# TensorE in written order through three of five MoE groups, local attention heads in joint stretches at fixed steps

## The chip, the cores and the metric

The kernel runs on one core of one Trainium2 chip. The metric is the device time of one execution in microseconds, as the median of several executions. The core's engines are TensorE (PE in the profile, with PEld for its weight loads), VectorE (DVE), ScalarE (ACT), GpSimd (POOL), and SyncE (SP), which issues the DMAs.

## The reference

Sparse attention over 4 batches, 8 heads, 576 positions and head size 64 is followed by two MoE-like blocks without routing. Four heads are local (a position sees the 32 up to itself), four are strided (it sees the earlier positions with the same residue modulo 32).

```python
mask_local = (rel >= 0) & (rel < stride)
mask_strided = (rel >= 0) & (pos[None, :] % stride == pos[:, None] % stride)
scores = np.where(masks[None, :, :, :], scores, -1000000000.0)
scores = scores - np.max(scores, axis=-1, keepdims=True)
attn = np.exp(scores)
attn = attn / (np.sum(attn, axis=-1, keepdims=True) + 1e-09)
out = np.matmul(attn, v)                                   # B, H, S, D

x = out.transpose(0, 2, 1, 3).reshape(B * S, H * D)        # 2304 x 512
h = x @ w_in                                               # first MoE block, d_ff 2048
x = (h - np.tanh(h)) @ w_out

rms = np.sqrt(np.mean(x * x, axis=-1, keepdims=True) + 1e-06)
xn = x / rms * rms_g                                       # second MoE block, d_ff 1536
g = xn @ w_gate
y = (g / (1.0 + np.exp(-g)) * (xn @ w_val)) @ w_out        # 2304 x 512
```

## The kernel before, in words

The 2304 tokens are cut into nine blocks of 256, numbered 0 to 8, and the blocks into five groups: (0, 1), (2, 3), (4), (5, 6), (7, 8). A group is 512 tokens wide, the middle one 256. While one group goes through the first MoE block, the attention of the next group's blocks is computed beside it; the last group has none beside it and prepares the second MoE block.

**The MoE step.** Group g takes 16 steps f (`unit`, L839). TensorE computes 12 matmuls into ps_h (`pe_h`, L643), ScalarE the tanh into tg, VectorE h minus tanh (tg, L659), ScalarE the high part of g (L665), VectorE its low part (g, L670), and TensorE 12 matmuls into ps_x (`pe_x`, L672) two steps later. ps_h has two buffers: the matmuls of step f + 2 wait for tg of step f. At the end of a group ps_x is evacuated (xe, L689 on VectorE, L691 on ScalarE).

**The local heads.** Each block has two units (`Local`, L218) and each unit three stages on TensorE. Stage s makes the scores (ps_s); VectorE then masks them and takes the maximum (L299, four times), ScalarE takes the exponential (L307), and VectorE normalises (ss, L311 and L312, and sm, L314). Stage p transposes the result (ps_p, L328), and ScalarE copies it out (L331). Stage v multiplies by the values (ps_v), and the result goes to the group's input xs, high part on ScalarE (L355), low part on VectorE (L356).

**The strided heads** of blocks 4 to 8 need no TensorE (`Strided`, L452). In a qk stretch GpSimd multiplies queries with keys into pr (L486) and VectorE sums each product into sc (L491). A softmax follows (smx, se, L501 to L509, with ScalarE's exponential at L505). In a pv stretch GpSimd multiplies with the values (L519), VectorE sums into so (L526), transposes (L534) and writes the low part into xs (L545) after ScalarE's high part (L544). pr has two buffers, so GpSimd is at most two products ahead of VectorE. Keys, queries and values have one buffer each. Block 4 has four short qk and pv stretches, one for each batch; blocks 5 and 6 have their qk in one long run, and then their pv; block 7 has one of each, and block 8.

**What sets the order.** The program is written step by step. In `unit`, `pe_work` stands between tanh and tg and takes stages from the list of the next group's local heads (`Work.run_pe`, L629), and `work` takes strided items (`Work.run`, L618). In the three middle groups `run_pe` is called with the number of steps that remain:

```python
def run_pe(self, k):
    n = -(-len(self.pe) // k) if k > 0 else len(self.pe)
    for _ in range(min(n, len(self.pe))):
        self.pe.pop(0)()
```

So one stage of one unit is written per step from step 0 on, in the order s, p, v of unit 0, then of unit 1. A scheduler then puts the instructions of every engine into an order of its own, from a simulated timeline. On the chip each engine takes its instructions in that order and waits at each for what it needs.

Of the kernel before, what the change touches and what calls it, by code (L numbers as in the profile page):

```python
# [25 lines left out]
def attn_moe_moe_kernel(  # L26
# [37 lines left out]
    NG = len(groups)  # L64
# [3 lines left out]
    def runs(s):  # L68

        r = []  # L70
        for i, (b, t) in enumerate(subs[s]):
            if r and r[-1][0] == b and r[-1][1] + r[-1][2] == t:
                r[-1][2] += 64
            else:
                r.append([b, t, 64, 64 * i])
        return r

    LB = 2
    EA = 2
    GC = 2  # L80
    PR = 6 * 64
    LANES = (5, 6, 7, 8)
# [22 lines left out]
    for s in range(len(subs)):  # L105
        if len(runs(s)) > 1 or s in LANES:
            _, t0, n, _ = runs(s)[0]
# [9 lines left out]
    class Weight:  # L117
        def __init__(self, kind, f):
            self.kind, self.f = kind, f
# [86 lines left out]
    def room(j, pool, name, words=512, **kw):  # L206

        if j < EA:
            return wts.tile([128, 1024], F32, tag="w", name=name)
        return pool.tile([128, words], F32, name=name, **kw)  # L210

    def copy(j, i):
        if j < EA and "aavaaaaa"[4 * j + i] == "v":
            return nc.vector.tensor_copy
        return nc.scalar.copy


    class Local:  # L218
# [9 lines left out]
        def load_qk(self):  # L228
            if self.j < EA:
                self.kT = wts.tile([128, 1024], F32, tag="w", name="kT")[:, :2 * self.kw]  # L230
                self.kT = self.kT.rearrange("r (p t) -> r p t", p=2)
                self.qz = wts.tile([128, 1024], F32, tag="w", name="qz").rearrange("r (u p t) -> r u p t", p=2, t=128)
                (nc.vector if self.j == 0 else nc.gpsimd).memset(self.qz[0:64, :, :, 64:128], 0.0)
                nc.gpsimd.memset(self.qz[64:128, :, :, 0:64], 0.0)
            else:
                self.kT = one.tile([128, 2, 4 * (W + 64)], F32, tag="kT", name="kT")[:, :, :self.kw]
                self.qz = qz
                if self.j == EA:
                    nc.gpsimd.memset(qz, 0.0)
            for b, t0, n, x0 in self.runs:  # L240
                for hh in range(2):
                    r = slice(64 * hh, 64 * hh + 64)
                    nc.sync.dma_start(
                        out=self.qz[r, x0 // 64:(x0 + n) // 64, :, r].rearrange("r u p t -> r (u p) t"),
                        in_=q_loc[b, r, t0 // 32:(t0 + n) // 32, :],
                    )
                o = self.at[x0 // 64]
                d = W if t0 == 0 else 0
                nc.sync.dma_start(out=self.kT[:, :, o + d:o + W + n], in_=k_loc[b, :, :, t0 - W + d:t0 + n])
# [112 lines left out]
    class Dense:  # L362
# [6 lines left out]
        def buf(self, tag, name, words):  # L369
            if self.j < EA:  # L370
                return wts.tile([128, 1024], F32, tag="w", name=name)
            return one.tile([128, words], F32, tag=tag, name=name)
# [79 lines left out]
    class Strided:  # L452
# [16 lines left out]
        def items(self):  # L469
# [5 lines left out]
            def flush():  # L475
                while pend:
                    pend.pop(0)()

            def prod(n, d):
                pr = att.tile([128, PR], F32, tag="pr", name="pr", bufs=2)  # L480
                return pr[:, :n * d].rearrange("l (c d) -> l c d", d=d)
# [31 lines left out]
            def pv_item(c, a, e, g0, gn):  # L513
                def go():
                    if c == g0 and a == 0:
                        flush()
                        self.o = one.tile([128, GC, D], F32, tag="so", name="so")
                    pr = prod(c + 1, e - a)
# [40 lines left out]
            qks.append((4, soft))  # L559
            for g0 in range(c0, c1, GC):  # L560
                gn = min(GC, c1 - g0)
                for c in range(g0, g0 + gn):
# [6 lines left out]
    loc = [Local(j) for j in range(len(subs))]  # L569
# [8 lines left out]
    class Work:  # L578


        def __init__(self, js):
            self.pe, self.st = [], []
            for j in js:
                pools = [(ps_m, "m"), (ps_h, "h")] if j < 1 else [(ps_m, "m")]
                kinds = [loc[j]]
                if isinstance(strd[j][0], Dense):
                    kinds += strd[j]
                else:
                    for o in strd[j]:
                        self.st += o.pvs if j in EARLY else o.items().qks + o.pvs  # L590
                    if j + 1 == EARLY[0]:
                        for o in (strd[i][0] for i in EARLY):
                            self.st += o.items().qks
                for nms in ("s,p,v" if j < EA else "spv").split(","):
                    for i in range(2):
                        for nm in nms:
                            for o in kinds:
                                self.pe.append(self.stage(o, i, nm, pools[len(self.pe) % len(pools)]))
# [28 lines left out]
                fn()  # L627

        def run_pe(self, k):  # L629
            n = -(-len(self.pe) // k) if k > 0 else len(self.pe)  # L630
            for _ in range(min(n, len(self.pe))):
                self.pe.pop(0)()


    def new_x(g):
        if g < NG:
            xs[g] = mid.tile([128, 2, 4, 512], F32R, tag="xs", name="xs")
            for k, j in enumerate(groups[g]):
                xh[j] = xs[g][:, :, :, SUB * k:SUB * k + SUB]
# [236 lines left out]
    for g, f, a, e in units:  # L876
        if g == 0:
            st1.to(2 * (f + 4))
        elif f == 0:
            new_x(g + 1)  # L880
            if g + 1 < NG:
                wks.append(Work(groups[g + 1]))
        if g == NG - 1 and f == 0:
            poolT.close()
            pbx = ctx.enter_context(tc.tile_pool(name="pbx", bufs=1, side="right", reuse_waits="tile"))
            gcol = pbx.tile([128, 4], F32, name="gcol")
            nc.sync.dma_start(out=gcol, in_=rms_g.rearrange("(c p) -> p c", p=128))
            ones = pbx.tile([128, 128], F32R, name="ones")
            nc.vector.memset(ones.bitcast(F32), 1.0)
        rem = FA - 1 - f  # L890
        wk = wks[-1]

        def pe_work():
            if f >= 2 or 0 < g < NG - 1:
                wk.run_pe(max(rem, 1))

        def work():
            if f >= 6 or 0 < g < NG - 1:
                wk.run(wk.st, max(rem, 1))

        unit(g, f, a, e, pe_work, work)
        if g == NG - 1:
            if f == 4:
                pg = prep(0, pbx)
            if pg is not None:
                next(pg, None)
# [109 lines left out]
```

## Time and profile before

| | us |
|---|---|
| median of 3 runs | 943.58 (943.53 to 944.5) |
| the profiled execution, its own time | 945.95 |
| its span in the profile | 943.1 |
| busy in the span: PE | 914.2 (97%) |
| DVE | 596.8 (63%) |
| ACT | 338.4 (36%) |
| POOL | 188.6 (20%) |

The span runs from the first to the last recorded instruction; the profiled execution took 2.85 us more than its span, and 2.37 us more than the median. Busy time is a sum over the whole span. POOL works only in its first half, and DVE is busier there than its share of the whole says; so the views by stretch of time are read beside the totals.

### The profile page before, as it was taken

To read this page: it belongs to the slowest core of one execution; us is meant where nothing else is said; L and a number is where in the kernel's file an instruction comes from. 1 tells how busy PE (TensorE), PEld (TensorE's weight loads), DVE (VectorE), ACT (ScalarE), POOL (GpSimd) and SP (SyncE) were. 2 spreads that over 40 slices of the span, in tenths; PEclk is the share of its full clock that TensorE was granted. 3 is DMA by queue.
4 is the path that set the end of the run, shared out by engine and by line. 5 is a ranking of instruction groups with operands and counts; after the bars stand their busy time and mean duration, and the time that the engine had idled before them with its cause. 6 is when DMAs were issued, how large, how long until landed. Compare 5 with 4: busy or idle time off the path is not lost.

```text
span 943.1 us, 13108 instructions
## 1 busy us (share of the span) xinstructions
PE 914.2 (97%) x4922; PEld 767.5 (81%) x4922; DVE 596.8 (63%) x1315; ACT 338.4 (36%) x778; POOL 188.6 (20%) x230
## 2 busy tenths in 40 slices
PE   6799999999889999999999999999999999999998
PEld 6688887888888877788888888888888888888897
DVE  4799997887899997959999782262125312421212
ACT  4776753322333432256656332222111211111211
POOL 2000024668856757500000000000000000000000
PEclk9799999999999999999999999999999999999999
DMA  9926424421312400065535201101010001000100
GB/s 216 339 112 214 122 73 132 123 80 35 107 36 63 89 27 5 1 223 179 174 107 188 90 23 45 44 4 42 1 45 0 23 1 45 1 0 1 46 1 22
DMA packets 47839, 72.62 MB, mean 77 GB/s; under 512 B 20768, under 2 KB 31392, under 8 KB 47776
## 3 DMA queue, kind: packets, MB, share of 16 engines
q1 hardware_dynamic: 47776, 71.80, 24.8%
q8 instruction: 38, 0.62, 0.3%
q14 instruction: 25, 0.20, 0.1%
HBM read 62.34 MB, written 9.44 MB: 76 GB/s over the span
## 4 chain that ended last, share of the span: by engine, by line
PE 57%; DVE 5%; POOL 2%; issue 1%; ACT 0%; POOLq 0%; DVEq 0%
PE ps_x L113 21%; PE ps_h L113 20%; PE ps_m L113 16%; DVE so L526 2%; POOL pr L486 1%; POOL pr L519 1%; DVE tg L659 1%; DVE g L670 1%; DVE sc L491 0%; DVE xs L545 0%; DVE sm L299 0%; DVE pr L534 0%; DVE sm L314 0%; DVE os L796 0%; ACT g L665 0%
## 5 line engine op out<-in xcount | busy, mean ns | idle before, releaser
L113 PE MATMUL ps_h<-xs,w 128*128 128x512 f32 (+1 forms) x984 | 222.1, 370 | 3.3 <-DVE tg L659 2.0
L113 PE MATMUL ps_x<-g,w 128*128 128x512 f32 (+1 forms) x984 | 218.1, 367 | 1.7 <-DVE xe L689 1.5
L113 PEld LDWEIGHTS ps_h<-xs,w 128*128 128x128 f32 x984 | 170.6, 191 | 33.6 <-DVE tg L659 3.1
L113 PEld LDWEIGHTS ps_x<-g,w 128*128 128x128 f32 x984 | 169.5, 189 | 32.2 <-issue 1.4
L771 DVE SCALAR_TENSOR_TENSOR s<-ps_m,s 128x512 f32<-128x512 f32 (+1 forms) x60 | 38.2, 637 | 219.8 <-PE ps_m L113 218.5
L113 PE MATMUL ps_h<-xn,w 128*128 128x512 f32 (+1 forms) x720 | 159.0, 369 | 0.0
L113 PE MATMUL ps_m<-xn,w 128*128 128x512 f32 (+1 forms) x720 | 158.6, 368 | 0.0
L113 PE MATMUL ps_x<-w,p 128*128 128x512 f32 x648 | 157.9, 391 | 0.0
L113 PEld LDWEIGHTS ps_h<-xn,w 128*128 128x128 f32 x720 | 126.8, 188 | 24.4
L113 PEld LDWEIGHTS ps_m<-xn,w 128*128 128x128 f32 x720 | 125.9, 188 | 23.1
L113 PEld LDWEIGHTS ps_x<-w,p 128*128 128x128 f32 x648 | 120.7, 188 | 25.6
L486 POOL TENSOR_TENSOR pr<-sk,sq 128x320 f32<-128x320 f32 (+2 forms) x104 | 98.5, 980 | 73.2 <-DMA sq<-in_q_str_dram 60.6
L519 POOL TENSOR_TENSOR pr<-sv,se 128x288 f32<-128x288 f32 (+11 forms) x108 | 83.1, 780 | 65.8 <-DVE so L526 31.3
L770 ACT ACTIVATE s<-ps_h 128x512 f32<-128x512 f32 (+1 forms) x60 | 33.3, 555 | 160.7 <-PE ps_h L113 160.7
L526 DVE TENSOR_REDUCE so<-pr 128x16 f32<-128x288 f32 (+12 forms) x108 | 81.5, 771 | 11.1 <-POOL pr L519 9.9
L665 ACT CAST g<-tg 128x512 fp32r<-128x512 f32 (+1 forms) x82 | 46.6, 568 | 116.2 <-DVE tg L659 116.0
L773 ACT CAST p<-s 128x512 fp32r<-128x512 f32 (+1 forms) x60 | 34.7, 578 | 120.7 <-DVE s L771 120.7
L491 DVE TENSOR_REDUCE sc<-pr 128x5 f32<-128x320 f32 (+2 forms) x104 | 50.9, 494 | 17.9 <-POOL pr L486 17.4
L670 DVE TENSOR_TENSOR g<-tg,g 128x512 fp32r<-128x512 f32 (+1 forms) x82 | 58.1, 708 | 5.3 <-ACT g L665 4.7
L133 ACT ACTIVATE ca<-raw 128x512 f32<-128x512 f32 x68 | 45.7, 674 | 39.5 <-DVE ct L141 14.5
L774 DVE TENSOR_TENSOR p<-s,p 128x512 fp32r<-128x512 f32 (+1 forms) x60 | 38.2, 637 | 25.1 <-ACT p L773 24.9
L659 DVE SCALAR_TENSOR_TENSOR tg<-ps_h,tg 128x512 f32<-128x512 f32 (+1 forms) x82 | 50.3, 614 | 5.1 <-ACT tg L654 5.0
(87 smaller groups left out, 703.0 us busy)
## 6 DMA issues: line engine op xcount, KB each, us to landing
raw<-in_w_out_dram SPq DMA_DIRECT2D x28, 512.0 KB, 5.6
raw<-in_w_in_dram SPq DMA_DIRECT2D x16, 512.0 KB, 7.8
raw<-in_w_gate_dram SPq DMA_DIRECT2D x12, 512.0 KB, 3.5
raw<-in_w_val_dram SPq DMA_DIRECT2D x12, 512.0 KB, 4.1
x2d<-xe SPq DMA_DIRECT2D x36, 128.0 KB, 2.4
x<-x2d SPq DMA_DIRECT2D x16, 256.0 KB, 4.1
out_dram<-o SPq DMA_DIRECT2D x16, 256.0 KB, 2.0
v<-in_v_loc_dram SPq DMA_DIRECT2D x14, 192.0 KB, 2.7
```

The source lines that it names most:

```text
L113: nc.tensor.matmul(out_, lhsT, rhs, start=start, stop=stop, skip_group_check=True)
L133: nc.scalar.mul(out=a, in_=hi.bitcast(F32), mul=2.0 ** -111)
L486: nc.gpsimd.tensor_tensor(out=pr, in0=self.k[:, a:e, :], in1=self.q[:, c - c0:c - c0 + 1, :].to_broadcast([128, e - a, D]), op=ALU.mult,)
L491: pend.append(lambda: nc.vector.tensor_reduce(out=s[:, c - c0, a:e], in_=pr, axis=AX.X, op=ALU.add))
L519: nc.gpsimd.tensor_tensor(out=pr, in0=self.v[:, 0:c + 1, a:e], in1=self.e[:, c - c0, 0:c + 1].unsqueeze(2).to_broadcast([128, c + 1, e - a ...
L526: pend.append(lambda: nc.vector.tensor_reduce(out=o[:, c - g0, a:e], in_=pr.rearrange("l c d -> l d c"), axis=AX.X, op=ALU.add))
L659: nc.vector.scalar_tensor_tensor(out=t, in0=h_of.pop((g, f, a)), scalar=WS, in1=t, op0=ALU.mult, op1=ALU.subtract)
L665: nc.scalar.copy(out=t[:, 0], in_=t_of[g, f, a])
L670: nc.vector.tensor_tensor(out=t[:, 1], in0=t_of.pop((g, f, a)), in1=t[:, 0].bitcast(F32), op=ALU.subtract)
L771: nc.vector.scalar_tensor_tensor(out=s, in0=r[1], scalar=WS, in1=s, op0=ALU.mult, op1=ALU.mult)
L773: nc.scalar.copy(out=t[:, 0], in_=s)
L774: nc.vector.tensor_tensor(out=t[:, 1], in0=s, in1=t[:, 0].bitcast(F32), op=ALU.subtract)
```

## The change

From the first step of the second group to the first step of the fifth, TensorE's instructions keep the order in which they are written; the other engines are ordered by the scheduler as before. For blocks 4 to 8 (`NEAR = 4`) a block's local heads are three entries in the list, each with both units: s of both, p of both, v of both. They are written at the steps that `STINT` names, and at no other: in the second group (block 4) steps 5, 8 and 11, in the third (blocks 5 and 6) steps 1, 4, 6 and 8, 11, 13, in the fourth (blocks 7 and 8) steps 1, 3, 5 and 8, 10, 12. No instruction of any engine is added or taken away.

```diff
+    NEAR = 4
+
+    STINT = {1: (5, 8, 11), 2: (1, 4, 6, 8, 11, 13), 3: (1, 3, 5, 8, 10, 12)}
...
+                if j >= NEAR:
+                    for nm in "spv":
+                        self.pe.append(lambda o=loc[j], nm=nm: [self.stage(o, i, nm, pools[0])() for i in range(2)])
+                    continue
                 for nms in ("s,p,v" if j < EA else "spv").split(","):
...
         def run_pe(self, k):
-            n = -(-len(self.pe) // k) if k > 0 else len(self.pe)
+            n = -(-len(self.pe) // k) if k > 0 else 0
...
         elif f == 0:
+            if g == 1:
+                order = ctx.enter_context(ExitStack())
+                order.enter_context(tc.manual_schedule(engines={mybir.EngineType.PE}))
+            if g == NG - 1:
+                order.close()
             new_x(g + 1)
...
         def pe_work():
-            if f >= 2 or 0 < g < NG - 1:
+            if g in STINT:
+                wk.run_pe(len(wk.pe) if f in STINT[g] else 0)
+            elif f >= 2:
                 wk.run_pe(max(rem, 1))
```

Three places of the engines' orders follow. First TensorE at the start of the second group, before (ps_h and ps_x are the MoE step, ps_s, ps_p and ps_v the stages of a local unit; one entry may stand for two records of the trace):

```order
L113 MATMUL ps_h<-xs,w 128x512 x12
L113 MATMUL ps_s<-kT,qz 128x96 x4
L113 MATMUL ps_h<-xs,w 128x512 x12
L113 MATMUL ps_x<-g,w 128x512 x12
L113 MATMUL ps_h<-xs,w 128x512 x12
L113 MATMUL ps_x<-g,w 128x512 x6
L113 MATMUL ps_h<-xs,w 128x512 x2
L328 MATMUL ps_p<-tab,sm 96x128 x4
L113 MATMUL ps_h<-xs,w 128x512 x4
L113 MATMUL ps_x<-g,w 128x512 x6
L113 MATMUL ps_h<-xs,w 128x512 x6
L113 MATMUL ps_x<-g,w 128x512 x6
```

And with the change, from step 4 of the group on:

```order
L116 MATMUL ps_h<-xs,w 128x512 x12
L116 MATMUL ps_x<-g,w 128x512 x12
L116 MATMUL ps_h<-xs,w 128x512 x12
L116 MATMUL ps_s<-kT,qz 128x96 x8
L116 MATMUL ps_x<-g,w 128x512 x12
L116 MATMUL ps_h<-xs,w 128x512 x12
L116 MATMUL ps_x<-g,w 128x512 x12
```

The stages no longer stand inside or between pieces of a block of 12; the scores of both units stand together behind the ps_h matmuls of step 5. With the change, every block of 12 in the three groups is whole.

Second, VectorE early in the third group, where the qk of block 6 ends and the pv of block 5 begins, before:

```order
L659 SCALAR_TENSOR_TENSOR tg<-ps_h,tg 128x256
L689 TENSOR_SCALAR xe<-ps_x 128x512
L491 TENSOR_REDUCE sc_96<-pr 128x5
L670 TENSOR_TENSOR g<-tg,g 128x256
L491 TENSOR_REDUCE sc_96<-pr 128x5
L689 TENSOR_SCALAR xe<-ps_x 128x512
L491 TENSOR_REDUCE sc_96<-pr 128x5
L491 TENSOR_REDUCE sc_96<-pr 128x6
L526 TENSOR_REDUCE so<-pr 128x32
L501 TENSOR_REDUCE smx<-sc_96 128x8
```

And with the change (the score operations of the two units, eight pairs, end with the first two rows; line numbers after the change are 3 to 12 higher):

```order
L302 ISA sm,nm<-ps_s,tab 128x96
L302 ISA nm 128x1
L494 TENSOR_REDUCE sc_96<-pr 128x5
L696 TENSOR_SCALAR xe<-ps_x 128x512
L314 TENSOR_SCALAR ss<-ss 128x4
L696 TENSOR_SCALAR xe<-ps_x 128x512
L494 TENSOR_REDUCE sc_96<-pr 128x6
L315 RECIPROCAL ss<-ss 128x4
L529 TENSOR_REDUCE so<-pr 128x32
L314 TENSOR_SCALAR ss<-ss 128x4
L504 TENSOR_REDUCE smx<-sc_96 128x8
L317 TENSOR_TENSOR sm<-sm,ss 128x384
```

Before, one unit's score operations stood some rows earlier and the other's came in the pv stretch; now both units of block 5 stand between the last sums of the qk stretch, and their normalisation among the first so. All the way back to the tg of that step there are four sc in both orders.

Third, VectorE where the strided work of block 8 ends, before, from the tg of step 14 of the fourth group on:

```order
L659 SCALAR_TENSOR_TENSOR tg<-ps_h,tg 128x512
L526 TENSOR_REDUCE so<-pr 128x21
L526 TENSOR_REDUCE so<-pr 128x22
L670 TENSOR_TENSOR g<-tg,g 128x512
L534 STREAM_TRANSPOSE pr<-so 128x128
L545 TENSOR_TENSOR xs<-pr,xs 128x2x64
L889 MEMSET ones 128x128
L659 SCALAR_TENSOR_TENSOR tg<-ps_h,tg 128x512
```

And with the change, from the tg of step 13 on:

```order
L666 SCALAR_TENSOR_TENSOR tg<-ps_h,tg 128x512
L529 TENSOR_REDUCE so<-pr 128x22
L529 TENSOR_REDUCE so<-pr 128x21
L677 TENSOR_TENSOR g<-tg,g 128x512
L529 TENSOR_REDUCE so<-pr 128x21
L529 TENSOR_REDUCE so<-pr 128x22
L537 STREAM_TRANSPOSE pr<-so 128x128
L548 TENSOR_TENSOR xs<-pr,xs 128x2x64
L901 MEMSET ones 128x128
L666 SCALAR_TENSOR_TENSOR tg<-ps_h,tg 128x512
L677 TENSOR_TENSOR g<-tg,g 128x512
```

The last xs of the strided heads now stands ahead of the tg of step 14 (the row behind the memset), and the g of that step comes after it; before, both stood ahead of the last xs.

## Rows read from the trace of the kernel before

**Rows 1.** Windows: us, busy time (x count) of PE, PEld, DVE, ACT, POOL, clock, DMA.

```profile
148.00:156.70 8.70, 8.44 (x38) 6.65 (x37) 6.92 (x20) 3.16 (x12) 5.46 (x7) 1.00 0.00 1
167.60:176.00 8.40, 8.16 (x39) 6.52 (x38) 7.94 (x22) 2.92 (x11) 5.47 (x7) 1.00 0.53 126
176.00:185.50 9.50, 9.50 (x57) 7.62 (x56) 7.63 (x19) 3.51 (x8) 6.23 (x6) 1.00 0.34 112
185.50:192.80 7.30, 7.30 (x34) 6.05 (x33) 6.49 (x11) 0.62 (x1) 5.48 (x7) 1.00 0.15 48
210.10:252.10 42.00, 39.33 (x210) 33.31 (x210) 32.18 (x77) 11.79 (x29) 36.93 (x41) 1.00 0.15 46
252.10:303.90 51.80, 47.30 (x420) 45.25 (x416) 49.51 (x127) 19.64 (x68) 30.45 (x40) 1.00 0.29 80
303.90:327.60 23.70, 23.70 (x135) 20.03 (x134) 21.47 (x61) 10.13 (x31) 19.03 (x21) 1.00 0.33 80
327.60:353.30 25.70, 24.25 (x128) 19.70 (x127) 23.89 (x49) 6.96 (x21) 15.37 (x20) 1.00 0.14 31
353.30:375.80 22.50, 22.04 (x129) 17.70 (x128) 17.61 (x45) 7.26 (x20) 17.93 (x21) 1.00 0.04 12
375.80:400.50 24.70, 23.55 (x102) 18.75 (x101) 22.76 (x38) 5.71 (x13) 14.53 (x19) 1.00 0.00 1
sum 252.50, PE 241.03 PEld 204.06 DVE 220.07 ACT 79.37 POOL 174.90; mean PE 18.54 PEld 15.70 DVE 16.93 ACT 6.11 POOL 13.45
```

**Rows 2.** Waits of PE, 148 to 400 us: us in total, times, longest.

```profile
PE ps_p L328 <- DVE sm L314: 6.8, 7, 2.0
PE ps_h L113 <- DVE tg L659: 1.8, 1, 1.8
PE ps_x L113 <- DVE xe L689: 1.5, 2, 1.0
```

**Rows 3.** Waits of DVE, 148 to 400.5 us.

```profile
DVE sc L491 <- POOL pr L486: 16.3, 42, 1.4
DVE so L526 <- POOL pr L519: 9.9, 16, 3.2
```

**Rows 4.** Timeline of DVE at the last strided result: start, us, what [idle before].

```profile
396.75 0.68 DVE L659 SCALAR_TENSOR_TENSOR tg<-ps_h,tg 128x512 f32<-128x512 f32 x1
398.91 0.68 DVE L670 TENSOR_TENSOR g<-tg,g 128x512 fp32r<-128x512 f32 x1
400.18 0.29 DVE L545 TENSOR_TENSOR xs<-pr,xs 128x128 fp32r<-128x128 f32 x1 [0.36 <-ACT xs L544]
```

**Rows 5.** Timeline of PE at the same place.

```profile
400.20 1.75 PE L113 MATMUL ps_h<-xs,w 128*128 128x512 f32 x6 [1.05 <-ACT xs L544]
401.79 1.52 PE L113 MATMUL ps_x<-g,w 128*128 128x512 f32 x6
```

**Rows 6.** Lines of DVE, 148 to 235 us: two local units and their results.

```profile
L299 DVE CUSTOM_DVE_ANT_0 sm<-ps_s,tab 128x96 f32<-128x96 f32 x8 | 1.6, 248 | 0.0
L311 DVE TENSOR_SCALAR ss<-ss 128x4 f32<-128x4 f32 x2 | 0.4, 216 | 0.0
L312 DVE RECIPROCAL ss<-ss 128x4 f32<-128x4 f32 x2 | 0.3, 163 | 0.0
L314 DVE TENSOR_TENSOR sm<-sm,ss 128x384 f32<-128x384 f32 x2 | 1.1, 537 | 0.0
L356 DVE TENSOR_TENSOR xs<-ps_v,xs 128x256 fp32r<-128x256 f32 x2 | 0.8, 415 | 0.0
```

**Rows 7.** Timeline of POOL: the wait inside the long qk stretch.

```profile
232.90 2.40 POOL L486 TENSOR_TENSOR pr<-sk,sq 128x256 f32<-128x256 f32 x3 [4.43 <-DMA sq<-in_q_str_dram]
```

**Rows 8.** Timeline of DVE at the turn from qk to pv, group three.

```profile
248.02 0.41 DVE L659 SCALAR_TENSOR_TENSOR tg<-ps_h,tg 128x256 f32<-128x256 f32 x1
252.12 0.66 DVE L526 TENSOR_REDUCE so<-pr 128x32 f32<-128x288 f32 x1
```

**Rows 9.** Lines of DVE, 210.1 to 252.1 us: one unit's normalisation.

```profile
L314 DVE TENSOR_TENSOR sm<-sm,ss 128x384 f32<-128x384 f32 x1 | 0.7, 705 | 0.0
```


## Prediction

> **What bounds the kernel now.** The table by windows comes first, because the totals hide it. I cut it where POOL turns from qk to pv and back [rows 1]. From 148 to 400.5 us, the part whose order changes, the clock stands at its upper level throughout, so PE is not slowed by it. PE is busy 241.0 of 252.5 us, so it stands idle for 11.5 us in all. If PE were the bound, that would be the prize, and the waits of PE say what ends the idle time: mostly seven waits of ps_p for sm, together 6.8 us, then one of ps_h for tg and two of ps_x for the evacuation [rows 2]. Program order with p written two or three steps behind s would take the first kind away.
>
> Whether that shortens anything depends on who is late, so the waits of DVE come next. In the whole part DVE waits for POOL, 16.3 us in qk and 9.9 us in pv [rows 3], and the answer has no row in which it waits for PE, not even for the matmuls behind tg. So PE is always ahead, and its stalls are the places where it has run so far ahead of DVE that it must wait: for sm, or else for a ps_h buffer a little later. The windows agree: in the two-block pv stretch DVE is busy 49.5 of 51.8 us, in those of blocks 7 and 8 23.9 of 25.7 and 22.8 of 24.7; in the long qk stretch POOL is busy 36.9 of 42.0 us, and one load of queries adds a wait of 4.4 us [rows 1, 7], which fills it. The part ends where the chain does: PE has half of the fifth group's first ps_h block done and waits for the last strided result [rows 4, 5].
>
> I therefore take POOL and DVE, in turn, as the bound from 148 to 400.5 us: qk stretches go at POOL's pace with room on DVE, pv stretches at DVE's pace. After that PE runs almost without a gap, and the rest of the kernel moves with the moment at which PE goes on.
>
> **The change, step by step** (minus is time gained). PE's work is the same; its order matters only where it changes what DVE and POOL do. The matmuls of PE itself lose a few interruptions, and that costs and gains nothing while PE waits for DVE. What moves on DVE is the local units. One unit costs DVE (1.6 + 0.4 + 0.3 + 1.1)/2 = 1.7 us: score operations 0.8, ss 0.35, sm 0.55; its result xs costs 0.4 [rows 6]. Moved out of a pv stretch this is gained; moved into a qk stretch it is hidden as far as DVE idles there.
>
> *Second group.* Before, the two units of block 4 lie in the first two pv stretches. The third has none and takes 7.3 us, the second 8.4, so -1.1; the first takes 8.7, of which an evacuation of about 0.7 stays, so -0.7 [rows 1]. Both units now stand at the end of the third qk stretch: 3.4 us, into a window in which DVE idles 9.5 - 7.6 = 1.9 us, so +1.5. Together -0.3.
>
> *The long qk stretch.* POOL's pace holds it, and the two late xs of block 4 are hidden. At its end DVE now has both units of block 5 among the last four sums. From the tg ahead of them to the first so it took 4.1 us [rows 8]; it now carries eight more or less hidden score operations (2 x 0.7 without their overlap), tg, g, four sums, two evacuations and two ss, in all about 5.4 us, and POOL, with two buffers, cannot run ahead. So +1.3.
>
> *The pv stretch of blocks 5 and 6.* Counting the order of DVE from its first so to its last, two tg, one g and four score operations leave it and one sm enters: 2 x 0.34 + 0.4 + 0.7 - 0.5 = 1.3 us (durations less the 0.08 that successive rows overlap). POOL stops once in here for a load, and the sm stood beside that pause, so 0.5 of it is not gained: -0.8.
>
> *Block 7.* In its qk stretch and softmax, 23.7 us, before, the second unit (1.7 us) stood in the softmax and ahead of the first so, where POOL has nothing to do; it moves up among the sums, where POOL sets the pace with 19.0 us. Some 0.6 of it filled the wait for the exponential, so -1.1. From the pv stretch the third unit leaves, a g and a result enter and a tg and a result leave: 1.3 on DVE, of which I take -1.0, because POOL's own pace gives some back. The qk stretch of block 8 takes in some 2.0 us, into a window with 22.5 - 17.6 = 4.9 us of room: +0.1.
>
> *The end.* The pv stretch of block 8 has one result more and one g less ahead of the point that counts, -0.1. But this point is another one. Before, tg of step 14 is done at 397.4 us and six of the fifth group's 12 ps_h matmuls run before the wait; PE goes on at 400.20 and reaches the next block at 401.79 [rows 4, 5]. Now that tg stands behind the last xs, and all 12 stand behind the tg. Half a block, 401.79 - 400.20 less the overlap, is 1.4 us: +1.4 with the end of DVE's row unchanged.
>
> Sum: -0.3 + 1.3 - 0.8 - 1.1 - 1.0 + 0.1 - 0.1 + 1.4 = **-0.5 us**. On the profiled execution this is 945.95 to 945.4; its own time lies 2.4 us above the median of the runs, so the forecast is 943.58 - 0.5 = **943.1 us**, no change that can be told: about 0.2%, 1.9 us, is what a measurement of this kernel can tell.
>
> The bounds. If every unit in a qk stretch is hidden and every list difference in pv is gained, the terms are -1.8, 0, -1.3, -1.7, -1.3, -0.5, -0.1, +1.4, in all -5.3. If every burst is paid in full and pv gives back most, they are +1.6, +1.8, -0.3, -0.3, -0.4, +1.5, 0, +1.5, in all +5.4. I stand near the middle, because the one measured case, the pv stretches with and without a unit, showed 0.7 and 1.1 of 1.7.
>
> **The rivals.** *A, PE was a bound after all.* If the seven waits for sm held back what DVE does next, they go, 6.8 us: 943.58 - 6.8 = 936.8. For it: they are the largest idle time of PE here. Against: no row of DVE ends with PE. It decides by whether DVE's idle time in the part falls with PE's. Chance 0.16.
>
> *B, the bursts are hidden* and the lower bound holds: 938.3. For it: DVE idles 32.4 us in the part, almost all for POOL. Against: the room lies between single sums, and the units come in one piece. Chance 0.20.
>
> *C, the joint bursts stop POOL*, the one that ends slower. Place: the ends of the qk stretches, where both units stand together. While DVE is in a burst it frees no product buffer and POOL stops after two. If the two stretches of blocks 7 and 8 pay what I put on the long one, 1.3 each in place of -1.1 and +0.1, the sum is -0.5 + 2.4 + 1.2 = +3.1: 946.7. It decides at the point where a burst outlasts two products, some 1.8 us (36.9 us for 41) [rows 1]; the score operations of both units are 1.4, with sm 2.5. For it also: sm took 0.54 us a piece beside block 4's short stretches and 0.70 in the long qk stretch [rows 6, 9]. Chance 0.22. The Trainium skill, "SBUF — State Buffer", section "Who interferes with whom", says that a VectorE instruction with two SBUF inputs contends with GpSimd's reads, and that the later one blocks fully. The trace agrees in direction, 0.70 against 0.54. By that rule each of the four sm that move into POOL's stretches would stop POOL for up to its own length; 4 x 0.55 makes the sum +1.7, 945.3 us, still within what cannot be told.
>
> **How the numbers follow.** Forecast 0.42, A 0.16, B 0.20, C 0.22. Faster by over 0.2% are A and B, 0.36; same 0.42; slower 0.22. The range takes the forecast, B and C with the spread around them, and leaves out A's better part and C's worse: 937.0 to 947.0 us. The likeliest case alone lies within 941.7 to 945.5.
>
> **What would show it.** Right: PE's waits for sm are gone or small, but PE's idle time in the part hardly falls and is ended by tg (ps_h) or the evacuation; DVE still never waits for PE; the first two pv stretches are near 7.5 us, the third qk stretch about 11; the first so of block 5 comes later by 1 to 2 us, and the last xs comes one tg earlier with PE waiting for that tg. Wrong: DVE idles less in the part by over 3 us, or PE reaches the fifth group before 398 us (A, B); or POOL's pauses at the ends of the qk stretches grow by over 1 us each (C). If PE in written order stands still at p for both units' sm, and DVE then waits for its matmuls, all of the above is wrong, because then PE has become part of the chain.

## The result, and the profile after

| | before | after |
|---|---|---|
| median of 6 runs, us | 943.62 (943.29 to 947.09) | 949.84 (948.61 to 952.13) |
| after / before, 95% interval | | 1.0061 [1.0043, 1.0079] |
| the profiled execution | 945.95 | 952.13 |
| its span | 943.1 | 950.4 |

The change costs 6 us, 0.6%. The forecast was 943.1 us, no change that can be told, and the range ended at 947.0: the prediction was wrong. Both profiled executions lie 2.3 us above their medians. Of the 7.3 us between the spans, 2.0 arise before the change acts: one and the same ps_x block at the end of the first group starts at 143.75 us in place of 141.73. The rest, 5.2, is what the traces can explain.

**Where it goes.** The same cut as in [rows 1], now strictly by VectorE: a pv stretch from its first so, a qk stretch from its first sc. The windows of the change (us, busy time of PE, PEld, DVE, ACT, POOL with counts, clock, DMA) are the second group's four pairs, the long qk stretch, pv of blocks 5 and 6, qk and pv of block 7, qk and pv of block 8:

```profile
151.52:212.03 60.51, 57.74 (x258) 47.00 (x257) 52.54 (x117) 18.38 (x47) 40.06 (x46) 0.97 0.31 93
212.03:254.61 42.58, 41.37 (x236) 34.87 (x234) 33.09 (x86) 12.96 (x36) 35.93 (x40) 1.00 0.19 54
254.61:308.43 53.82, 46.11 (x413) 45.02 (x412) 50.94 (x117) 17.90 (x59) 30.15 (x40) 0.94 0.26 78
308.43:333.49 25.06, 23.89 (x120) 20.13 (x121) 22.05 (x63) 10.30 (x33) 17.73 (x21) 0.93 0.28 76
333.49:357.41 23.92, 23.92 (x133) 19.65 (x133) 21.37 (x36) 5.59 (x14) 15.67 (x20) 1.00 0.12 34
357.41:381.07 23.66, 23.66 (x118) 19.91 (x117) 19.73 (x58) 8.92 (x28) 19.25 (x21) 1.00 0.03 6
381.07:405.24 24.17, 22.54 (x126) 18.17 (x126) 21.83 (x38) 4.91 (x12) 14.64 (x19) 1.00 0.00 1
```

The same cut of the kernel before gives 61.31, 41.21, 51.66, 23.82, 25.56, 22.66 and 24.65 us; the change adds 2.85 us, most of it in one line, the pv stretch of blocks 5 and 6: +2.2. That line before:

```profile
252.12:303.78 51.66, 47.16 (x419) 45.12 (x416) 49.39 (x127) 19.52 (x68) 30.45 (x40) 1.00 0.29 79
```

DVE is busy 1.55 us longer in it and idle 0.6 us longer. The first, third and fourth line of after also show a second thing that was not there before: a clock below 1.00.

The rest stands at the end. VectorE and TensorE where the strided work ends, in place of [rows 4, 5]:

```profile
399.81 0.68 DVE L666 SCALAR_TENSOR_TENSOR tg<-ps_h,tg 128x512 f32<-128x512 f32 x1
404.95 0.29 DVE L548 TENSOR_TENSOR xs<-pr,xs 128x128 fp32r<-128x128 f32 x1 [0.36 <-ACT xs L547]
405.45 0.69 DVE L666 SCALAR_TENSOR_TENSOR tg<-ps_h,tg 128x512 f32<-128x512 f32 x1
```

```profile
400.54 3.01 PE L116 MATMUL ps_h<-xs,w 128*128 128x512 f32 x12 [1.63 <-DVE tg L666]
403.39 2.88 PE L116 MATMUL ps_x<-g,w 128*128 128x512 f32 x12
406.20 3.01 PE L116 MATMUL ps_h<-xs,w 128*128 128x512 f32 x12
409.05 1.30 PE L116 MATMUL ps_x<-g,w 128*128 128x512 f32 x5
```

Before, the ps_x block of step 14 started 1.32 us after the last xs was done (401.79 less 400.47). Now it starts at 409.05, the last row, 3.81 us after it (405.24), and the rows run without a gap behind the first: PE is not waiting for the last strided result any more, it is itself late, one step behind, since it stood 1.63 us for the tg of step 13. That is +2.5. With the 2.85 it makes 5.3.

**What ends PE's idle time** from 143.7 to 405.3 us (total, times, longest), and what DVE waits for from 151.5 us on:

```profile
PE ps_h L116 <- DVE tg L666: 6.0, 3, 2.3
PE ps_x L116 <- ACT xe L698: 5.2, 2, 4.2
PE ps_x L116 <- DVE xe L696: 3.0, 3, 1.9
```

```profile
DVE sc L494 <- POOL pr L489: 17.1, 42, 1.8
DVE so L529 <- POOL pr L522: 8.9, 17, 2.6
DVE xs L548 <- ACT xs L547: 2.6, 7, 0.4
```

Beside [rows 2] the waits for sm are gone, 6.8 us to nothing, and waits for tg and for the evacuation came, 3.3 us to 14.2. DVE's waits for POOL are near those of [rows 3]. It waits for PE only once, by way of tanh, for 0.7 us.

**The turn of the groups.** The largest stand of PE, with what ScalarE did then:

```profile
252.88 1.17 PE L116 MATMUL ps_x<-g,w 128*128 128x256 f32 x6 [1.06 <-ACT xe L698]
254.20 0.62 PE L116 MATMUL ps_x<-g,w 128*128 128x256 f32 x3
258.98 1.01 PE L116 MATMUL ps_x<-g,w 128*128 128x256 f32 x3 [4.17 <-ACT xe L698]
259.79 2.55 PE L116 MATMUL ps_h<-xs,w 128*128 128x256 f32 x11
```

```profile
257.35 0.31 ACT L508 ACTIVATE se<-se 128x128 f32<-128x128 f32 x1 [3.44 <-DVE se L505]
258.33 0.60 ACT L698 ACTIVATE xe<-ps_x 128x512 f32<-128x512 f32 x1 [0.68 <-DMA x2d<-xe]
```

In written order the third group's first ps_x block comes as soon as its g is there, while the second group's accumulators still wait to be evacuated; the order of the kernel before had put ps_h matmuls in front of such a block. The fourth evacuation is the late one. It stands on ScalarE behind the strided softmax's exponential, which waits for VectorE, but its row names something else as the last to end its wait, 0.68 us after the exponential: a DMA that writes an evacuated piece out (x2d<-xe). Evacuated pieces and tg share three buffers in the program, so the fourth piece takes the buffer of the first, once that one has been written out. The DMA queue, after and before:

```profile
252.78 0.33 SPq L464 DMA_DIRECT2D sk<-in_k_str_dram  x1
253.21 0.38 SPq L465 DMA_DIRECT2D sq<-in_q_str_dram  x1
253.68 6.08 SPq L704 DMA_DIRECT2D x2d<-xe  x8
```

```profile
249.06 2.29 SPq L697 DMA_DIRECT2D x2d<-xe  x5
251.49 0.35 SPq L461 DMA_DIRECT2D sk<-in_k_str_dram  x1
```

After, two strided loads of 512 and 256 KB go ahead of the pieces. The first piece's two DMAs, issued at 253.7 and 254.1 us, landed 4.2 and 4.1 us later, just ahead of the fourth evacuation at 258.33. Before, the first piece's landed after 1.7 and 1.8 us. In six of the runs below (experiments 1, 3, 4, 5, 9 and 13) the loads stand directly ahead of all the pieces in the same way, and the fourth evacuation begins 4.1 to 4.7 us after the end of the third; in the kernel before and where its third group is kept (8, 10 and 14) it is 0.6, and in the rest, where the loads come earlier or later, at most 2.7. So the order of the DMA queue is a part of this stand. No run changes it alone, and what it is worth is open.

**The clock.** Windows in three places: behind a stand of PE of 1.90 us for the evacuation, from inside the one of 4.17 us above, and behind one of 2.06 us for a tg:

```profile
163.50:166.50 3.00, 3.00 (x8) 2.32 (x8) 2.73 (x5) 0.62 (x1) 2.13 (x3) 0.50 0.40 132
255.60:262.00 6.40, 3.02 (x14) 3.02 (x15) 6.40 (x17) 1.99 (x5) 2.95 (x5) 0.50 0.66 229
310.20:313.30 3.10, 3.10 (x9) 2.42 (x8) 2.73 (x7) 0.41 (x1) 3.10 (x5) 0.50 0.00 0
```

The granted clock is at its lower level there, half of the upper, and 1.00 throughout this part before. A block of 12 at 512 wide then takes 4.61 us behind the third stand in place of 2.88. From that ps_x block at the end of the first group to one and the same point of the fifth, PE's account is before:

```profile
141.73:414.99 273.26, 261.79 (x1504) 221.37 (x1503) 232.83 (x535) 87.66 (x241) 174.90 (x206) 1.00 0.24 69
```

and after:

```profile
143.75:422.25 278.50, 264.02 (x1504) 225.03 (x1503) 236.24 (x536) 88.96 (x242) 174.28 (x206) 0.98 0.23 68
```

So the same 1504 matmuls are busy 2.2 us longer and idle 14.5 in place of 11.5 us: 3.0 + 2.2 = 5.2. The 2.2 us are a balance. PE is busy 9.1 us in the three windows, and at the upper level half of that, over 4.5 us, would not be there (an estimate from these rows and the clock's two levels); so the whole blocks of 12 must give over 2 us back. DVE's work (one row more) is busy 3.4 us longer, and that asks for a closer look at single instructions.

**sm.** Lines of DVE in the pv stretch of blocks 5 and 6: the normalisation took 1085 ns a piece, against 0.55 us in the same stretch before:

```profile
L317 DVE TENSOR_TENSOR sm<-sm,ss 128x384 f32<-128x384 f32 x4 | 4.3, 1085 | 0.0
```

Two of the four, with POOL's products beside them:

```profile
257.18 1.09 DVE L317 TENSOR_TENSOR sm<-sm,ss 128x384 f32<-128x384 f32 x1
287.85 1.15 DVE L317 TENSOR_TENSOR sm<-sm,ss 128x384 f32<-128x384 f32 x1
```

```profile
257.13 0.72 POOL L522 TENSOR_TENSOR pr<-sv,se 128x320 f32<-128x320 f32 x1 [1.10 <-DVE so L529]
287.81 0.78 POOL L522 TENSOR_TENSOR pr<-sv,se 128x352 f32<-128x352 f32 x1 [1.49 <-DVE ss L315]
```

The product was under way, by 0.05 and 0.04 us, when sm began, and sm ended 0.42 us (258.27 less 257.85) and 0.41 us (289.00 less 288.59) after the product did. So it stood until the product was over and then did its work. Before, one sm shows the other side:

```profile
261.86 0.55 DVE L314 TENSOR_TENSOR sm<-sm,ss 128x384 f32<-128x384 f32 x1
262.33 0.89 DVE L670 TENSOR_TENSOR g<-tg,g 128x256 fp32r<-128x256 f32 x1
```

```profile
262.03 0.91 POOL L519 TENSOR_TENSOR pr<-sv,se 128x273 f32<-128x273 f32 x1 [1.25 <-DVE so L526]
```

Here sm was first by 0.17 us and took its 0.55; the product beside it took 0.91 us, where six of the seven others of its shape take 0.65 to 0.67 us, and the next instruction, g, stood until the product's end. The Trainium skill, "SBUF — State Buffer", section "Who interferes with whom", says just this: of a VectorE instruction with two SBUF inputs and a GpSimd instruction that reads SBUF, the one that issues first goes on and the other blocks fully. What decides the price is the place in VectorE's order, to within an instruction. An so frees a product buffer and POOL begins; the sm of 261.86 us stands directly behind an so and was ahead of that product, while all four in the change's stretch come one or two short instructions (ss, smx, se, tg) later and met it. Six of the ten sm of the change took over 0.9 us, the ten together 9.2 us against 6.2. The kernel before had it already, in a milder form: four of its ten took 0.71, 0.80, 0.82 and 0.61 us, and each of these ended 0.41 to 0.42 us behind a product that was under way when it began.

### The profile page after: what moved, and what is told of

Its sections match the earlier page's. It is cut to its first block, busy times and chain, and to the rows that moved or that the text cites. A ratio compares the mean times of both kernels' runs of the same rounds, so it can differ in the third digit from the quotient of the medians.

```text
span 950.4 us, 13110 instructions
## 1 busy us (share of the span) xinstructions
PE 915.3 (96%) x4922; PEld 770.3 (81%) x4922; DVE 599.8 (63%) x1315; ACT 339.1 (36%) x778; POOL 188.0 (20%) x230
## 4 chain that ended last, share of the span: by engine, by line
PE 57%; DVE 2%; POOL 0%; ACT 0%; issue 0%; ACTq 0%
PE ps_x L116 21%; PE ps_h L116 21%; PE ps_m L116 16%; DVE so L529 1%; POOL pr L522 0%; DVE g L677 0%; DVE tg L666 0%; ACT pT L334 0%; DVE xs L548 0%; DVE os L803 0%; DVE xs L359 0%; DVE sc L494 0%; ACT g L672 0%; DVE pr L537 0%; ACT se L508 0%
## 5 line engine op out<-in xcount | busy, mean ns | idle before, releaser
L116 PEld LDWEIGHTS ps_h<-xs,w 128*128 128x128 f32 x984 | 174.1, 195 | 37.8 <-DVE tg L666 8.0
L661 ACT ACTIVATE tg<-ps_h 128x512 f32<-128x512 f32 (+1 forms) x82 | 44.4, 542 | 39.2 <-PE ps_h L116 38.5
```

The source lines that it names most:

```text
L116: nc.tensor.matmul(out_, lhsT, rhs, start=start, stop=stop, skip_group_check=True)
L661: nc.scalar.activation(out=t, in_=h_of[g, f, a], func=ACTF.Tanh, scale=WS)
```

## The experiments

Each is timed in 5 rounds beside the kernel before; the ratio is to that, with its 95% interval. The first two take the change apart.

**1. The joint steps alone.**

```diff
...
-                order.enter_context(tc.manual_schedule(engines={mybir.EngineType.PE}))
...
```

> Keeps the joint stages at the fixed steps and gives TensorE's order back to the scheduler. Theory O (TensorE in written order is what costs: it stands 4.2 us at the evacuation and the clock falls behind it): the 6.2 us go, 943 to 945 us. Theory J (the joint stages cost: two units in one burst hold DVE and POOL, and sm runs beside a product at 1.0 us in place of 0.55): most of it stays, 947 to 950 us, and sm keeps a median near 1.0 us.

946.11 us, 1.0019 [1.0011, 1.0028]; ten sm took 7.0 us. Between the two ranges, so neither theory as it stood: the steps alone cost 1.8 us, the written order on top of them 4.

**2. The written order alone.**

```diff
-    NEAR = 4
+    NEAR = 99
...
-                wk.run_pe(len(wk.pe) if f in STINT[g] else 0)
+                wk.run_pe(rem)
```

> Keeps TensorE's written order in the three groups and writes the local heads as before, one stage of one unit per step. Theory O: the wait at the evacuation and the falls of the clock stay, 947 to 951 us. Theory J: 943 to 945 us, sm back at a median near 0.55 us, the two-block pv stretch back at some 51.7 us.

959.05 us, 1.0163 [1.0145, 1.0181], worse than either theory allowed. PE's waits in it, 141 to 417 us:

```profile
PE ps_p L331 <- DVE sm L317: 16.5, 7, 4.3
PE ps_p L331 <- ACT xs L547: 6.3, 1, 6.3
```

With p written one step behind s, PE stands at p until sm is done, and all of the MoE behind it. Now DVE does wait for PE, by way of tanh: 4.6 us at tg, four times, up to the last strided result, where the kernel before has no such wait. So the order is what hurts, and the fixed steps are what makes it bearable. What is left to find is which part of the order.

**3. sm in four pieces**, each with a column as its second factor, in the changed kernel.

```diff
-                nc.vector.tensor_tensor(
-                    out=sm[:, a:e, :, :w], in0=sm[:, a:e, :, :w],
-                    in1=ss[:, a:e].unsqueeze(3).to_broadcast([128, e - a, 2, w]), op=ALU.mult,
-                )
...
+                        nc.vector.tensor_scalar_mul(
+                            out=sm[:, u, p, :], in0=sm[:, u, p, :], scalar1=ss[:, u, p:p + 1])
```

> The changed kernel with sm of blocks 4 to 8 written as four multiplications by a column (one wide input each) in place of one instruction with two wide inputs. Theory J, in the form that the long sm is what costs: four pieces take 0.7 to 0.8 us together whether POOL is at work or not, some 3 us of the loss go, 946 to 947.5 us. Theory O: within 0.5 us of the changed kernel, 949 to 950.5 us.

954.10 us, 1.0105 [1.0091, 1.0118]: a miss. The premise was wrong, pieces with one wide input stand too:

```profile
254.55 1.15 DVE L319 TENSOR_SCALAR sm<-sm,ss 128x96 f32<-128x96 f32 x4
257.04 0.79 DVE L319 TENSOR_SCALAR sm<-sm,ss 128x96 f32<-128x96 f32 x4
```

The first four met a product that ended at 255.10 us, the others one that was nearly over. The same section of the Trainium skill says that a tensor_scalar can enter a two-port mode, in which it contends as well. And undisturbed pieces cost more than the whole, 0.81 us where no product was at work; the ten sets of four took 12.5 us together, against 9.2. This run does not tell the theories apart.

**4. All evacuations of the second group on VectorE**, so that none stands behind the exponential.

```diff
-            if c % 2 == 0:
+            if c % 2 == 0 or g == 1:
```

> The changed kernel with all four evacuations of the second group on VectorE, so that none stands behind the strided softmax's exponential on ScalarE; DVE gets two more operations of 0.7 us there. Theory O: the wait of 4.2 us and the fall of the clock after it go, 945 to 947 us. Theory J: the wait goes, but DVE's chain has 1.4 us more, 949.5 to 951.5 us.

950.81 us, 1.0070 [1.0058, 1.0083], as the changed kernel and within theory J's range. The wait of 4.2 us is one of 4.3 us for VectorE's evacuation. Who evacuates is not the point: the two loads stand ahead in the DMA queue here too, the piece whose buffer the fourth evacuation takes had not landed before 256.1 us, and VectorE began the evacuation at 256.61.

**5. The turns free:** the written order only from step 4 to step 14 of each group.

```diff
-                order.enter_context(tc.manual_schedule(engines={mybir.EngineType.PE}))
...
+        if g in STINT and f == 4:
+            order.enter_context(tc.manual_schedule(engines={mybir.EngineType.PE}))
+        if g in STINT and f == FA - 1 or g == NG - 1 and f == 0:
+            order.close()
```

> The changed kernel with the written order only from step 4 to step 14 of each of the three groups; around the turns of the groups TensorE's order is the scheduler's again. Theory T (the loss is made at the turns, where the first ps_x block in written order waits for the evacuation of the group before, and the clock falls behind that wait): the waits of ps_x for the evacuation, 8.2 us, fall under 3 us and 3 to 5 of the 6.2 us go, 945 to 947 us. Theory I (the loss is made inside the groups, by the order of s, p, v and tg): 949 to 951 us.

949.84 us, 1.0060 [1.0048, 1.0073]: no change, and theory T seems dead. The waits for the evacuation fell from 8.2 only to 5.8 us, but the end was mended: PE's ps_x block of step 14 came 1.32 us after the last xs, as before. In its place the pv stretch of blocks 5 and 6 grew to 55.7 us: 14 tg and 13 g fell into that stretch in place of 12 and 12, since PE was less late, and DVE's idle time in it went from 2.9 to 4.2 us, mostly for POOL. The time only moved from PE to the strided chain. Two costs lay side by side, and the next runs were made to remove them one by one and together.

**6 and 7. The third group's stages later**, with and without the written order.

```diff
-    STINT = {1: (5, 8, 11), 2: (1, 4, 6, 8, 11, 13), 3: (1, 3, 5, 8, 10, 12)}
+    STINT = {1: (5, 8, 11), 2: (3, 5, 7, 9, 11, 13), 3: (1, 3, 5, 8, 10, 12)}
```

> The changed kernel, written order kept, with the third group's stages at steps 3, 5, 7, 9, 11, 13 in place of 1, 4, 6, 8, 11, 13, so that the first scores no longer stand at the turn. Theory T in the form that the burst of two units delays the evacuation: the wait of 4.2 us falls to 2 us or less, and 2 to 4 us go, 946 to 948 us. If the evacuation is late for another reason (the strided softmax at the same place): 949 to 951 us.

> The same later steps with TensorE's order left to the scheduler, to be held against the joint steps alone (1.9 us over the kernel before). If its one wait of 2.5 us at the evacuation, with the fall of the clock behind it, comes from the scores at step 1: 942 to 944.5 us. If not: 945.5 to 947 us.

951.95 us, 1.0086 [1.0073, 1.0100], and 949.38 us, 1.0067 [1.0052, 1.0083], outside all the ranges. Without the written order that is slower than with the scores at step 1; with it, the interval just touches that of the changed kernel. The long qk stretch gave back its 1.2 us (41.5 and 41.4), but the scores of block 5 now fall into the pv stretch, and that took 59.8 and 58.0 us. The first scores at step 1 were not badly placed. That 58.0 came without the written order speaks for the strided chain: there no order of PE was fixed.

**8. Only the second group joint**, the other groups as before, and no written order.

```diff
-    STINT = {1: (5, 8, 11), 2: (1, 4, 6, 8, 11, 13), 3: (1, 3, 5, 8, 10, 12)}
+    STINT = {1: (5, 8, 11)}
...
-                if j >= NEAR:
+                if j == NEAR:
...
```

> Only block 4 has joint stages, at steps 5, 8 and 11 of the second group; the third and fourth group as before, and no written order. In the three profiles with joint stages, the second group's strided work took 0.8 us less than before. If that gain is carried to the end: 942.8 to 943.8 us. If the third group, which starts earlier, waits it away: 944 to 945 us.

945.29 us, 1.0008 [1.0000, 1.0017]. The second group took 60.45 us, 0.86 less, but the pv stretch of blocks 5 and 6 took 52.6, 1.0 more, with DVE as busy as before and idle 0.8 us longer: waited away, as the second case said, and a little more.

**9 to 11. sm on ScalarE**, in the changed kernel, the kernel before, and the joint steps alone.

```diff
...
+                        nc.scalar.activation(
+                            out=sm[:, u, p, :], in_=sm[:, u, p, :], func=ACTF.Copy, scale=ss[:, u, p:p + 1])
...
```

> The changed kernel with sm of blocks 4 to 8 on ScalarE (four activations with a column as scale, some 1.4 us a unit there) in place of VectorE's one instruction. Theory S (the strided chain of POOL and DVE still sets the time, and sm, which in this kernel starts while a product of POOL is under way, waits for the product's end: 1.0 to 1.28 us in place of 0.55): VectorE loses 9.2 us of sm, 4.3 of them in the two-block pv stretch; that stretch falls from 53.8 to 49 to 51 us, the whole to 943 to 947 us. If the loss is TensorE's written order and not DVE: within 1 us of the changed kernel, 949 to 951 us.

> The kernel before with sm on ScalarE in the same way. Theory S: VectorE loses 6.2 us of sm, of which 1.6 in the two-block pv stretch and 0.55 in that of block 7 count in full, the rest is partly hidden: 941 to 943.5 us. If DVE is not what sets the time: 944 us and more, since sm comes 0.9 us later per unit.

> The joint steps alone (scheduler's order) with sm on ScalarE. Theory S: 942 to 944.5 us, 2 to 4 us less than the joint steps alone. If not: 945.5 to 947.5 us.

947.62 us, 1.0040 [1.0028, 1.0053]; 942.95 us, 0.9991 [0.9982, 0.9999]; 945.99 us, 1.0017 [1.0008, 1.0025]. The first lies between its two ranges, the second in theory S's range but by less than I hold for tellable; the third is a miss, no less than the joint steps alone (sm was 7.0 us there, not 9.2, and DVE's idle time grew by 7.4 us while its work shrank by 8.1).

In the changed kernel the seven stretches together came down from +2.85 to +0.7 us against before. 1.7 us of this is the qk stretch of block 7, where two sm had taken 1.28 and 1.13 us. The pv stretch of blocks 5 and 6, for which 49 to 51 us was expected, came down only from 53.8 to 53.3, though 4.3 us of sm had left it: DVE was idle 1.9 us longer in it, and its g and xs took 1.2 us more, since more of them now met the products. So sm as the cause of that stretch's growth is not shown by this run. PE was also late at the end, by 4.38 us in place of 1.32, and these are its waits:

```profile
PE ps_x L116 <- ACT xe L704: 7.1, 2, 3.7
PE ps_x L116 <- DVE xe L702: 3.4, 4, 1.9
PE ps_h L116 <- DVE tg L672: 3.1, 2, 2.5
```

So with the chain relieved PE's stand at the turns became the limit, the mirror of experiment 5.

**12. The two units of a stage one step apart**, in written order.

```diff
...
-                        self.pe.append(lambda o=loc[j], nm=nm: [self.stage(o, i, nm, pools[0])() for i in range(2)])
+                        for i in range(2):
+                            self.pe.append(self.stage(loc[j], i, nm, pools[0]))
```

> The changed kernel, written order kept, with the two units of a stage written one step apart in place of together (second group: scores at 5 and 6, p at 8 and 9, v at 11 and 12, and so on), so that no burst on DVE has two units. Theory B (the joint burst stops POOL): the long qk stretch and that of block 7 lose about 1 us each, 946 to 948.5 us. If the price is sm's place beside a product, which this does not govern: anything from 947 to 952 us, with sm's median telling.

951.17 us, 1.0065 [1.0052, 1.0078]. The joint burst itself is not the cost: without it the long qk stretch still took 42.25 us and that of block 7 25.8. This was rival C's mechanism, and it falls in that form for these two stretches; the qk stretch of block 8 did come back, from 23.66 to 22.83 us. The ten sm took 7.3 us here in place of 9.2, and PE stood 7.1 us for the evacuation in place of 8.2: both costs were smaller, and the time was the same. The pv stretch of blocks 5 and 6 took 55.3 us; four more score operations and an evacuation fell into it. So the two costs are not all that sets this stretch: what the new order puts into it counts as well.

**13. Both costs removed:** sm on ScalarE and the turns free.

> The changed kernel with both: sm of blocks 4 to 8 on ScalarE, and TensorE's written order only from step 4 to step 14 of each of the three groups. Theory P (two separate costs: sm beside POOL's products on VectorE, and TensorE standing at the turns, which left it 3 us behind the last strided result when sm was on ScalarE): with both gone the time is that of the joint steps with sm on ScalarE, 945 to 946.5 us, and TensorE goes on within 1.5 us of the last strided result. If the stages inside the groups in written order still cost: 947 to 949 us.

944.97 us, 1.0009 [1.0000, 1.0018]. PE's account over the same piece of work, beside the two above:

```profile
140.34:413.94 273.60, 263.23 (x1504) 223.88 (x1503) 230.43 (x525) 97.74 (x282) 171.47 (x206) 0.99 0.23 69
```

PE is idle 10.4 us, the waits for the evacuation are 4.4 us, and the step-14 block comes 1.34 us after the last xs. Of 0.61% are left 0.09%: alone the one edit took away nothing and the other 0.21%, together 0.52%. The move of sm takes 0.09% off the kernel before as well (experiment 10); held against that, 0.18% is left. In the pv stretch of blocks 5 and 6 the move of sm was worth 0.6 us while PE stood at the turns, and with the turns free 3.3 us (55.67 to 52.35).

**14. A faster kernel than both?** Joint stages in the second group, no written order, sm on ScalarE.

> Joint stages in the second group only, no written order, sm on ScalarE: the second group's gain of 0.8 us on top of the kernel before with sm on ScalarE (0.9991 of before). If the two add up: 941.5 to 943 us, the fastest here. If the third group waits the gain away, as it did with sm on VectorE: 943 to 944.5 us.

942.31 us, 0.9986 [0.9972, 0.9999]: the fastest here, by 0.14%, less than what I hold for tellable.

The stretches of the runs on which the argument rests (us; first so or sc to the next; last column: from the end of the last xs to the ps_x block of step 14):

| | 2nd group | qk 5, 6 | pv 5, 6 | qk 7 | pv 7 | qk 8 | pv 8 | end | sum less before |
|---|---|---|---|---|---|---|---|---|---|
| before | 61.31 | 41.21 | 51.66 | 23.82 | 25.56 | 22.66 | 24.65 | 1.32 | |
| after | 60.51 | 42.58 | 53.82 | 25.06 | 23.92 | 23.66 | 24.17 | 3.81 | +5.3 |
| joint steps alone | 60.48 | 42.56 | 52.74 | 24.74 | 23.32 | 24.04 | 24.79 | 1.32 | +1.8 |
| turns free | 60.18 | 42.50 | 55.67 | 25.22 | 23.31 | 24.02 | 24.77 | 1.32 | +4.8 |
| sm on ScalarE | 61.25 | 42.60 | 53.26 | 23.36 | 23.96 | 23.42 | 23.73 | 4.38 | +3.8 |
| both | 61.37 | 42.58 | 52.35 | 24.08 | 24.27 | 22.19 | 24.92 | 1.34 | +0.9 |

## Why the prediction was wrong

*What bounds the kernel* held, as far as the kernel before goes. In before and in ten of the fourteen variants the step-14 block comes 1.31 to 1.34 us after the last strided result, whether that was at 399 or at 410 us: the chain of POOL and DVE sets the end of this part there. In the changed kernel it does so only together with PE.

*The steps that failed:*

- *The pv stretch of blocks 5 and 6*, -0.8, measured +2.2. The count of what leaves and enters was right (sm four in place of three, two tg and one g fewer), but the price of sm was taken from rows where it ran by itself, 0.55 us (the two "beside block 4's short stretches" had no product under way when they began); in the new order it took 1.085, four times 0.53 more, and one more sm, 2.7 us in all. The removal of sm did not give this back while PE stood at the turns (experiment 9), so how much of the +2.2 is due to sm alone is not shown. The sentence on the Trainium skill's rule gave +1.7 for four such sm and had the right contention, but the wrong way round: it let sm stop POOL, and POOL stopped sm. I ranked it under C and did not carry it into the sum, since I had read only 0.70 against 0.54; the same trace has 0.80 and 0.82. POOL's waits in that stretch of the kernel before (11.9 us for so, 19 times) would have told that it begins right behind an so.
- *The end*, +1.4, measured +2.5. I had PE wait for the tg of step 14; it stood already for that of step 13, and being in written order it had the rest of one block and the whole of the next still to do when the last xs was done.
- "The matmuls of PE itself lose a few interruptions, and that costs and gains nothing while PE waits for DVE": this left out the turns. The kernel before had two waits for the evacuation, 1.5 us [rows 2]; that the scheduler had been putting ps_h matmuls in front of them was not priced as something the written order takes away. They became five, 8.2 us, the longest of them with the DMA queue's new order in it, and three times the clock went to its lower level at a stand; with the whole blocks' saving taken off, PE was busy 2.2 us longer. The forecast had the clock at the upper level throughout.
- Block 7 (-1.1 and -1.0) measured +1.2 and -1.6, the qk of block 8 (+0.1) +1.0: in the qk stretch of block 7 the two sm took 1.28 and 1.13 us, and without them it was back at 23.4 us (experiment 9).

*What was right:* the waits of PE for sm go and others take their place; the second group gains (-0.8, -0.3 forecast); the long qk stretch loses (+1.4, +1.3 forecast, though with the units one step apart it still lost 1.0, so it was not the joint burst); the last xs moves one tg ahead. The first pv stretches took 7.75 and 7.06 us (about 7.5 forecast), the third qk stretch 11.3 (about 11).

*The rivals.* A and B are out: nothing got faster. C named the side, and the places: the qk stretches of blocks 7 and 8, for which it had 1.3 us each, lost 1.2 and 1.0. Its mechanism is not what block 7 shows: the loss stayed without the burst (experiment 12) and went with sm (experiment 9), so POOL's products stopped sm; for block 8 it is not excluded. C's 946.7 us also had no stand of PE in it. The last sentence of the prediction's list, that PE in written order may become part of the chain, is what came true at the turns and at the end, though it named p.

What stays open: the 1.8 us of the joint steps alone, which sm on ScalarE did not take away; what the place of the two loads in the DMA queue costs; and how much of each variant comes from the scheduler's new orders of the other engines, which every edit brings along.

## What to carry to other kernels

A written order saves the waits it was drawn up against and brings back those that a scheduler had quietly filled: list the places where it now puts other work in front of a late operand, above all the turn from one accumulator to the next. When two chains run near each other, removing one cost alone can show little or nothing; remove them together before calling a theory dead. And price a VectorE instruction with two SBUF inputs by what GpSimd does at its new place, not by its mean at the old one. And read to the end what a late instruction waited for: the evacuation that seemed to wait for an exponential was released by a DMA.

## What the runs showed of the hardware

An sm of VectorE, with two inputs in SBUF, that begins after a product of GpSimd has begun ends a fixed piece after that product (0.41 to 0.42 us, in six cases of the changed kernel and four of the kernel before); one that begins first takes its own time (0.55 us), and the product is the longer one (0.91 us). Pieces with one wide input and a column stand beside a product too (four took 1.15 us beside one, 0.81 us with none).

Seven stands of PE for sm, of up to 2.0 us, left the clock at 1.00 in the kernel before; in the changed kernel it went to 0.50 behind stands of 1.90 and 2.06 us and inside one of 4.17 us, and stayed there beyond the end of that stand.

A DMA of 128 KB that was issued right behind two of 512 and 256 KB landed after 4.1 to 4.2 us, and one that was issued ahead of them after 1.7 to 1.8 us.
